# Value products of the last six chunks taken over two chunks, 512 columns at a time

## The chip, the cores and the metric

The kernel runs on one core of a Trainium2 chip. The metric is the time of one execution on the device in microseconds (us), the median of several runs. Engines are named as the profile names them: PE is TensorE (PEld its weight loads), DVE is VectorE, ACT is ScalarE, POOL is GpSimd, SP is SyncE, which issues every transfer.

## The reference

Inputs are `q`, `k`, `v` of 4 batches, 8 heads, 768 positions, 64 values, and per head a decay `lam`. The first half is attention with decay, by blocks of 64 positions and a carried state; the second gates a projection by a causal filter of five taps.

```
for b in range(nb):                       # blocks of 64 positions
    intra = (qb @ kb^T * Dmask) @ vb      # Dmask[i, j] = lam^(i-j), i >= j
    inter = (qb * lam_pow) @ kv_state
    out[b] = intra + inter
    kv_state = lam^64 * kv_state + (kb * rev_pow)^T @ vb
x = out with the heads side by side       # (4, 768, 512)
gate = sigmoid(sum_k conv_w[k] * x shifted by 4 - k positions)
val = x @ w_val                           # 512 x 512, the value products
result = (gate * val) @ w_out             # 512 x 512, the output products
```

The two weights come in float64.

## The kernel before

The work is cut into 12 chunks: chunk i holds 128 positions of two batches (6 chunks for one pair of batches, then 6 for the other). Two chunks in a row make a unit (`UNIT` = 2, six units). Per chunk, TensorE computes the scores (pieces `s`, L470), the intra part (`ia`, L510), the inter part from the state (`in`, L547) and the state's addition (`st`, L572), all in small 64 by 64 products for chunks 3 to 11; VectorE masks the scores (`m`, L490) and updates the state (`up`, L581), GpSimd scales q and k (`qd`, `kd`) and fades the state (`fd`, L584). ScalarE copies the result x out of its bank (`x`, L634).

The second half multiplies in three terms: x is split into a high part (`xh`, ScalarE, L659) and a rest (`xl`, GpSimd, L669), the weights likewise, and a product is high by high, rest by high, high by rest. A value piece `v.i.f` (L734) makes column block f (128 of 512) of chunk i: 12 products whose stationary operand is a 128 by 128 block of the weight and whose moving operand is 256 columns, the 2 x 128 positions of the chunk. Two blocks share a bank. The filter runs per unit and block over 512 elements: the first tap on ScalarE (`t.un.ct.0`, L693), four more on VectorE (`t.un.ct.1` to `4`, L695), then the sigmoid (`sg`, L700). For chunks 6 to 11 (`DIRECT`) the gate is multiplied in place in the bank (`ap`, VectorE, L748), the gated value is cast to its high part (`hh`, ScalarE, L771) and the rest is subtracted (`hl`, VectorE, L774); the bank is free after that. An output piece `p.i.b.j.u` (L797) makes half of the contraction of one batch's 128 positions, moving 512 columns of `w_out`; the evicted bank (`ev`, ACT, L804) is stored by SP (`o`, L807). The very last output is made and stored in two halves of 256 columns.

Order and buffers are written out by hand. `ORDER` (L32) names every piece once, in the order in which all engines get their instructions, and after a colon the buffers that a piece takes (`u0` to `u3` are four of the eight banks, `hs`, `val`, `xs` and others lie in the on-chip buffer). Each engine runs its pieces in that order and waits where a piece needs another engine's result or a buffer not yet free. `Plan.run` (L114) walks the list:

```
        for piece in ORDER.split():
            name, _, takes = piece.partition(":")
            k = self.at[name]
            assert k not in done and done.issuperset(self.work[k][3]), name
```

Of the kernel before, what the change touches and what calls it, by code (L numbers as in the profile page):

```python
# [7 lines left out]
F32 = mybir.dt.float32  # L8
# [4 lines left out]
ALU = mybir.AluOpType  # L13
# [16 lines left out]
H_DVE = (6, 7, 8, 9, 10, 11)  # L30
# [8 lines left out]
xh.1:xs1 wv.1.0.w up.1.0 x.1 qd.2.1:qd1 v.0.1 wv.1.0.v m.2.1.0:A0 wv.1.0.h fd.1.0 m.2.0.0 s.2.1:u3,u1 pb.0.0:val0 xl.1  # L39
# [3 lines left out]
wo.1.1.s wo.0.0.s pb.1.0:val3 qd.3.0:qd1 x.2:x1 wo.1.1.w s.3.0:s0 xh.2:xs0 v.1.2:u1 m.3.1.0:A1 qd.3.1 m.3.0.0  # L43
# [3 lines left out]
wo.0.1.r t.0.3.4 pb.2.1:val2 m.5.1.0:A1 sg.0.0 ia.4.0:xp0 wo.0.1.s xh.3:xs1 in.4.0 wo.0.1.n st.4:u0,u3 sg.0.3 xl.3  # L47
# [6 lines left out]
t.1.2.2 ia.6.0:xp0 p.1.0.0.0:u3 pk.6 t.1.2.3 t.1.3.0:u1 qd.6.0 xh.5:xs1 t.1.3.1 kd.7.0 p.1.0.0.1 t.1.3.2 fd.6.0  # L54
t.1.2.4 in.6.1 ev.1.0.0:o0 m.7.0.0:A1 xl.5 ia.6.1 hh.0.1:hs1 o.1.0.0 t.1.3.3 p.1.1.0.0:u3 ld.8.2:ld2 x.6:x0 up.6.1
ld.8.0 t.1.3.4 t.1.1.0:u2 p.1.1.0.1 hi.2 sg.1.3 t.1.1.1 qd.7.1:qd1 t.1.1.2 v.5.2:u1 ev.1.1.0:o1 fd.6.1 t.1.1.3 hh.0.0
o.1.1.0 ld.9.2:ld1 sg.1.2 qd.7.0 v.5.3 t.1.1.4 ld.9.0 t.1.0.0:u3 sg.1.1 t.1.0.1 hl.0.0 ia.7.0:xp0 pb.5.1:val1 t.1.0.2
in.7.0 st.7:u0,u2 hl.0.1 t.1.0.3 t.1.0.4 p.0.0.0.0:u1 kd.8.1 up.7.0 sg.1.0 ap.2.1 t.2.1.0:u3,g0 fd.7.0 p.0.0.0.1
t.2.1.1 hh.2.1:hs0 m.7.1.0 p.0.1.0.0:u0 ev.0.0.0:o0 ap.2.0 xh.6:xs0 t.2.1.2 p.0.1.0.1 hh.2.0 t.2.1.3 hl.2.0 ap.3.0
v.5.0:u1 ev.0.1.0:o1 t.2.2.0:u0 qd.8.0:qd0 o.0.1.0 t.2.1.4 in.7.1 ia.7.1 t.2.2.1 sg.2.1 s.8.0:s0 hl.2.1 ld.10.0:ld0  # L60
t.2.3.0:u3 t.2.2.2 o.0.0.0 x.7 v.5.1 up.7.1 qd.9.0:qd1 t.2.2.3 p.2.0.0.0:u2 t.2.2.4 pb.5.0 qd.8.1 t.2.3.1 hh.3.0:hs1
sg.2.2 ap.3.1 p.2.0.0.1 kd.8.0 t.2.0.0:u1 m.8.0.0:A0 hh.3.1 t.2.0.1 p.2.1.0.0:u0 ev.2.0.0:o1 kd.9.0 t.2.3.2 o.2.0.0
m.8.1.0 p.2.1.0.1 kd.9.1 t.2.0.2 hl.3.1 t.2.0.3 s.9.0:s0 ev.2.1.0:o0 t.2.0.4 hl.3.0 ia.8.0:xp0 t.2.3.3 in.8.0 sg.2.0
st.8:u2,u0 t.2.3.4 fd.7.1 m.9.0.0:A1 sg.2.3 p.3.1.0.0:u1 qd.9.1 up.8.0 ap.4.0 p.3.1.0.1 hi.3 m.9.1.0 hh.4.0:hs0 fd.8.0
ap.4.1 t.3.1.0:u3,g1 in.8.1 hl.4.0 ev.3.1.0:o1 ia.8.1 t.3.1.1 o.3.1.0 p.3.0.0.0:u2 x.8:x1 ld.11.2:ld2 up.8.1
# [12 lines left out]
sg.4.1 hh.8.1:hs1 p.6.0.0.1 t.5.0.0:u3,g1 hl.8.1 t.5.3.0:u1 v.9.0:u2 t.5.3.1 ev.6.0.0:o0 o.6.0.0 v.9.1 v.8.0:u0 ap.9.0
t.5.3.2 hh.9.0:hs0 v.8.1 hl.9.0 v.9.2:u2 xh.11:xs1 ap.8.0 hh.8.0 v.9.3 hl.8.0 p.8.1.0.0:u0 ap.9.1 hh.9.1 p.8.1.0.1
xh.10:xs0 hl.9.1 t.5.3.3 xl.10 p.9.1.0.0:u2 ev.8.1.0:o0 t.5.3.4 o.8.1.0 t.5.0.1 sg.5.3 o.7.1.0 p.9.1.0.1 t.5.2.0:u0  # L80
xl.11 t.5.2.1 p.8.0.0.0:u1 t.5.2.2 ev.9.1.0:o0 t.5.2.3 p.8.0.0.1 t.5.2.4 p.9.0.0.0:u2 ev.8.0.0:o1 t.5.1.0:u1 o.8.0.0
o.9.1.0 sg.5.2 p.9.0.0.1 t.5.1.1 t.5.1.2 v.11.2:u0 ev.9.0.0:o1 t.5.1.3 o.9.0.0 t.5.0.2 v.11.3 t.5.0.3 t.5.1.4
v.10.2:u2 ap.11.1 t.5.0.4 hh.11.1:hs1 v.10.3 sg.5.1 sg.5.0 v.10.0:u1 ap.10.1 hh.10.1:hs0 v.10.1 v.11.0:u3 ap.10.0
hl.10.1 hh.10.0 v.11.1 hl.10.0 p.10.1.0.0:u2 ap.11.0 hh.11.0 p.10.1.0.1 hl.11.0 hl.11.1 p.10.0.0.0:u1 ev.10.1.0:o0
o.10.1.0 p.10.0.0.1 p.11.1.1.0:u3 ev.10.0.0:o1 p.11.1.1.1 p.11.0.0.0:u0 ev.11.1.1:o0 o.11.1.1 o.10.0.0 p.11.0.0.1
p.11.1.0.0:u2 ev.11.0.0:o0 p.11.1.0.1 o.11.0.0 f.2:u1 ev.11.1.0:o1 o.11.1.0
# [41 lines left out]
def decay_attention_then_gated_conv(  # L128
# [262 lines left out]
    for i in range(N):  # L391
# [256 lines left out]
        xs_buf, hs_buf = Buf("xs"), Buf("hs")  # L648
# [66 lines left out]
    for i, s, un, j, xs_buf, hs_buf, g_buf, t_g, t_xs in gated:  # L715
        gs = lambda u, un=un, j=j: xu[un]["g"][:, HU * u : HU * (u + 1), j]
        t_h, val_buf = {}, Buf("val")
        h_in = i in H_DVE
        assert i >= DIRECT or not h_in
        h_bufs = {}  # L720
        for u in range(2):
            us = slice(HU * u, HU * (u + 1))
            vp_buf = Buf("u")
            h_bufs[u] = vp_buf if h_in else g_buf

            def value(f, u=u, s=s):
                x_hi, x_lo = (s[n].rearrange("p t b i -> p t (b i)") for n in ("x_hi", "x_lo"))
                if f == 0:
                    s["vp", u] = bank("vp", [P, HU, W])
                fs = slice((HU * u + f) * P, (HU * u + f + 1) * P)  # L730
                n_mm = 0
                for ct in range(NT):
                    for w, xx in ((wv.hi, x_hi), (wv.hi, x_lo), (wv.lo, x_hi)):
                        nc.tensor.matmul(  # L734
                            s["vp", u][:, f, :], w[:, ct, fs], xx[:, ct, :],
                            start=n_mm == 0, stop=n_mm == 3 * NT - 1,
                        )
                        n_mm += 1

            def put_by(u=u, us=us, s=s):  # L740
                if "val" not in s:
                    s["val"] = buf("val", "val", [P, NT, W])
                nc.scalar.copy(s["val"][:, us], s["vp", u])

            def apply(u=u, us=us, s=s, i=i, gs=gs):
                val = s["vp", u] if i >= DIRECT else s["val"][:, us]
                s["h", u] = s["vp", u] if i in H_DVE else gs(u)
                nc.vector.tensor_tensor(out=s["h", u], in0=val, in1=gs(u), op=ALU.mult)  # L748

            t_gu = [t_g[ct] for ct in range(HU * u, HU * (u + 1))]  # L750
            t_v = None
            for f in range(HU):
                t_v = add(
                    f"v.{i}.{HU * u + f}", "PE", lambda f=f, g=value: g(f),
                    [t_v, t_xs, *wv.done[HU * u + f], *(t_gu if i >= DIRECT else ())], [vp_buf, xs_buf],
                )
            if i >= DIRECT:
                t_h[u] = add(f"ap.{i}.{u}", "DVE", apply, [t_v, *t_gu], [vp_buf, g_buf])
            else:
                t_v = add(f"pb.{i}.{u}", "ACT", put_by, [t_v], [vp_buf, val_buf])  # L760
                t_h[u] = add(f"ap.{i}.{u}", "DVE", apply, [t_v, *t_gu], [val_buf, g_buf])

        t_hs = []
        for u in range(2):
            us = slice(HU * u, HU * (u + 1))

# [92 lines left out]
```

## Time and profile before

| | |
|---|---|
| median of 3 runs | 209.81 us (209.22 to 210.12) |
| the profiled execution's own time | 209.46 us |
| its span, first to last instruction | 207.7 us |
| TensorE busy | 201.4 us, 97% of the span |
| VectorE, GpSimd, ScalarE busy | 153.6, 116.4, 115.2 us |
| transfers | 36.17 MB, 174 GB/s |

The profile shows one execution. Busy time is when an engine worked; TensorE's products overlap, so the duration of one is longer than the step from its start to the next one's. The chain that ended last follows, back from the end, what released each piece of work. Windows are stretches of the span, in us from its start.

### The profile page before, as it was taken

The numbers are of one execution on the slowest core, as the hardware profiler recorded it, in microseconds if no ns is written. First come the engines' busy times: TensorE is split into PE (matmuls) and PEld (weight loads), VectorE is DVE, ScalarE is ACT, GpSimd is POOL, SyncE is SP. The second block draws the span as 40 slices with busy tenths as digits, with TensorE's granted clock in tenths as the row PEclk, the third lists the DMA queues.
The fourth block names the chain that finished last, engine by engine and source line by source line (L and its number), as shares of the span: only waits on it lengthen the run. The fifth ranks groups of instructions, "written<-read, shape, count | busy, mean of one in ns | idle before, by whom it ended". The sixth has DMA issues, their size and how long they took to land.

```text
span 207.7 us, 7755 instructions
## 1 busy us (share of the span) xinstructions
PE 201.4 (97%) x3460; PEld 179.7 (87%) x3460; DVE 153.6 (74%) x240; ACT 115.2 (55%) x218; POOL 116.4 (56%) x103
## 2 busy tenths in 40 slices
PE   7879899998999999999999999999999999999995
PEld 7569799998999988989797889999789998899883
DVE  5697997989586989999999993465858457683500
ACT  2177779779664967577546394323456336432211
POOL 5176592887887599849999569952440006300000
DMA  5999999703787005985506465120110102220022
GB/s 181 425 419 426 426 429 426 319 6 90 320 300 312 5 3 144 412 358 159 202 3 199 166 218 238 54 104 3 51 54 3 51 0 82 94 81 0 3 95 107
DMA packets 7953, 36.17 MB, mean 174 GB/s; under 512 B 1136, under 2 KB 1392, under 8 KB 4336
## 3 DMA queue, kind: packets, MB, share of 16 engines
q1 hardware_dynamic: 7920, 35.68, 44.6%
q8 instruction: 27, 0.44, 0.9%
q14 instruction: 6, 0.05, 0.1%
HBM read 29.38 MB, written 6.29 MB: 172 GB/s over the span
## 4 chain that ended last, share of the span: by engine, by line
PE 87%; DMA 7%; SPq 2%; DVE 1%; POOL 1%; issue 1%; ACT 0%
PE vp L734 34%; PE op L797 33%; DMA w_raw<-in_w_val 7%; PE xp L510 5%; PE xp L547 4%; PE s L470 4%; PE st L572 4%; SPq L337 1%; PE xp L525 1%; POOL wv_lo L302 1%; PE so L460 1%; PE xp L536 0%; PE st L564 0%; PE fill L205 0%; DVE w_em L260 0%
## 5 line engine op out<-in xcount | busy, mean ns | idle before, releaser
L695 DVE SCALAR_TENSOR_TENSOR acc<-x,conv_sb,acc 128x512 f32<-128x512 f32 x96 | 70.9, 753 | 6.5 <-ACT acc L693 4.7
L797 PE MATMUL op<-wo_hi,hs 128*128 128x512 f32 (+1 forms) x200 | 61.1, 388 | 0.0
L734 PE MATMUL vp<-x_hi,wv_hi 128*128 128x256 f32 x192 | 55.6, 290 | 0.0
L734 PE MATMUL vp<-x_hi,wv_lo 128*128 128x256 f32 x192 | 54.3, 283 | 0.7 <-POOL wv_lo L302 0.7
L734 PE MATMUL vp<-x_lo,wv_hi 128*128 128x256 f32 x192 | 54.2, 282 | 0.0
L797 PEld LDWEIGHTS op<-wo_hi,hs 128*128 128x128 f32 x200 | 36.0, 188 | 7.3
L797 PE MATMUL op<-wo_lo,hs 128*128 128x512 f32 (+1 forms) x100 | 38.4, 384 | 0.0
L734 PEld LDWEIGHTS vp<-x_hi,wv_hi 128*128 128x128 f32 x192 | 36.4, 190 | 1.5 <-issue 0.2
L669 POOL TENSOR_TENSOR x_lo<-x,x_hi 128x1024 fp32r<-128x1024 f32 x10 | 23.9, 2400 | 23.8 <-ACT x_hi L659 23.8
L734 PEld LDWEIGHTS vp<-x_hi,wv_lo 128*128 128x128 f32 x192 | 36.4, 190 | 0.9 <-POOL wv_lo L302 0.9
L734 PEld LDWEIGHTS vp<-x_lo,wv_hi 128*128 128x128 f32 x192 | 36.4, 190 | 0.3
L804 ACT COPY o<-op 128x512 f32<-128x512 f32 (+1 forms) x25 | 14.3, 571 | 24.9 <-PE op L797 23.1
L584 POOL TENSOR_TENSOR sdec<-state,qdec_c 128x512 f32<-128x512 f32 x17 | 19.3, 1138 | 12.0 <-DVE state L581 11.9
L420 POOL TENSOR_TENSOR qd<-ld,qdec_c 128x512 f32<-128x512 f32 (+1 forms) x18 | 23.0, 1286 | 2.6 <-DMA ld<-in_qkv 2.6
L797 PEld LDWEIGHTS op<-wo_lo,hs 128*128 128x128 f32 x100 | 18.8, 188 | 3.9
L700 ACT ACTIVATE g<-acc 128x512 f32<-128x512 f32 x24 | 14.2, 601 | 13.4 <-DVE acc L695 13.2
L774 POOL TENSOR_TENSOR hs<-g,hs 128x512 fp32r<-128x512 f32 x12 | 15.9, 1335 | 8.8 <-ACT hs L771 8.8
L748 DVE TENSOR_TENSOR vp<-vp,g 128x512 f32<-128x512 f32 x12 | 8.4, 699 | 15.5 <-PE vp L734 15.5
L771 ACT CAST hs<-vp 128x512 fp32r<-128x512 f32 x12 | 7.0, 587 | 20.8 <-DVE vp L748 20.8
L693 ACT ACTIVATE acc<-x,conv_sb 128x512 f32<-128x512 f32 x24 | 16.6, 694 | 1.8 <-DVE state L581 1.5
L581 DVE TENSOR_TENSOR state<-st,sdec 128x512 f32<-128x512 f32 x17 | 11.7, 687 | 7.5 <-PE st L572 5.7
L634 ACT COPY x<-xp 128x512 f32<-128x512 f32 x24 | 12.9, 592 | 5.0 <-PE xp L510 4.9
(71 smaller groups left out, 295.7 us busy)
## 6 DMA issues: line engine op xcount, KB each, us to landing
ld<-in_qkv SPq DMA_DIRECT2D x24, 1024.0 KB, 8.4
out<-o SPq DMA_DIRECT2D x23, 256.0 KB, 2.4
w_raw<-in_w_val SPq DMA_DIRECT2D x2, 1024.0 KB, 11.3
w_raw<-in_w_out SPq DMA_DIRECT2D x2, 1024.0 KB, 14.0
out<-o SPq DMA_DIRECT2D x2, 128.0 KB, 1.7
conv_raw<-in_conv_w SPq DMA_DIRECT2D x1, 20.0 KB, 10.4
lam_bc<-in_lam SPq DMA_DIRECT2D x1, 4.0 KB, 1.6
```

The source lines that it names most:

```text
L420: nc.gpsimd.tensor_tensor(out=s["qd"][:, hs, ms], in0=lds[i]["qT"][:, u].rearrange("p h (m i) -> p h m i", m=2)[:, :, ms], in1=qdec[:, hs, ...
L581: nc.vector.tensor_tensor(out=state, in0=s["st"][m], in1=sdec, op=ALU.add)
L584: nc.gpsimd.tensor_tensor(out=sdec, in0=state, in1=qdec_c[:, :, n - 1 : n].to_broadcast([P, H, D]), op=ALU.mult)
L634: nc.scalar.copy(*blocks(s["x"], b))
L669: nc.gpsimd.tensor_tensor(out=s["x_lo"], in0=s["x"], in1=s["x_hi"].bitcast(F32), op=ALU.subtract)
L693: nc.scalar.mul(to, src, w)
L695: nc.vector.scalar_tensor_tensor(out=to, in0=src, scalar=w, in1=to, op0=ALU.mult, op1=ALU.add)
L700: nc.scalar.activation(xu[un]["g"][:, ct].rearrange("p u (b i) -> p b u i", b=NB2), xu[un]["acc", ct].rearrange("p b (u i) -> p b u i", u= ...
L734: nc.tensor.matmul(s["vp", u][:, f, :], w[:, ct, fs], xx[:, ct, :], start=n_mm == 0, stop=n_mm == 3 * NT - 1,)
L774: (nc.vector if h_in else nc.gpsimd).tensor_tensor(out=s["h_lo"][:, us], in0=s["h", u], in1=s["h_hi"][:, us].bitcast(F32), op=ALU.subtract,)
L797: nc.tensor.matmul(s["op", b, j][:, cols], hh[:, ft, ts], w[:, ft, cols], start=ft == 0 and n == 0, stop=ft == NT - 1 and n == 2,)
L804: nc.scalar.copy(s["o", b, j][:, cols], s["op", b, j][:, cols])
```

## The change

The value products of units 3, 4 and 5 (chunks 6 to 11) are made for both chunks of a unit at once. A wide piece `V.un.f` has 12 products of 512 columns into a whole bank, and needs x of both chunks split. The gating, cast and subtraction of a wide group (`apw`, `hhw`, `hlw`) take one column block of both chunks, 512 elements as before. The split x of a unit lies in one tile of twice the size (`xs`), the high part of a unit's gated value in one `hs` buffer, its rest in two `val` buffers. `ORDER` is the same for the first 411 pieces but for the `xs` buffers; from the 412th on (at 104 us in the profile) it is new, for every engine and for SP's stores and loads. `value` is now L728, gating L774, the subtraction L810, the output products L837, the store L847.

```diff
-H_DVE = (6, 7, 8, 9, 10, 11)
+WIDE = (3,4,5)
...
-v.10.2:u2 ap.11.1 t.5.0.4 hh.11.1:hs1 v.10.3 sg.5.1 sg.5.0 v.10.0:u1 ap.10.1 hh.10.1:hs0 v.10.1 v.11.0:u3 ap.10.0
...
+t.5.0.4 sg.5.0 t.5.2.0:u0 xl.11 p.9.1.0.1 t.5.1.4 t.5.2.1 t.5.2.2 t.5.2.3 V.5.0:u3 t.5.2.4 ev.9.1.0:o1 sg.5.1 V.5.1:u2
...
-        def split_x(s=s, now=now, blocks=blocks):
-            at = plan.slot("xs")
-            s["x_hi"] = work.tile([P, NT, NB2, C], F32R, name="x_hi", tag=f"{at}_hi", bufs=1)
-            s["x_lo"] = work.tile([P, NT, NB2, C], F32R, name="x_lo", tag=f"{at}_lo", bufs=1)
+        def split_x(un=un, j=j, s=s, now=now, blocks=blocks):
+            if "x_hi" not in xu[un]:
+                at = plan.slot("xs")
+                for part in ("hi", "lo"):
+                    xu[un][f"x_{part}"] = work.tile(
+                        [P, NT, UNIT, NB2, C], F32R, name=f"x_{part}", tag=f"{at}_{part}", bufs=1
+                    )
+            s["x_hi"], s["x_lo"] = (xu[un][n][:, :, j] for n in ("x_hi", "x_lo"))
...
+    def value(f, to, hi, lo):
+
+        fs = slice(f * P, (f + 1) * P)
+        n_mm = 0
+        for ct in range(NT):
+            for w, xx in ((wv.hi, hi), (wv.hi, lo), (wv.lo, hi)):
+                nc.tensor.matmul(to, w[:, ct, fs], xx[:, ct], start=n_mm == 0, stop=n_mm == 3 * NT - 1)
+                n_mm += 1
...
+        wide, direct = un in WIDE, UNIT * un >= DIRECT
+        if wide and j == 0:
+            continue
...
+        groups = [(f,) for f in range(NT)] if wide else [tuple(range(HU * u, HU * (u + 1))) for u in range(2)]
...
+                if f == fs[0]:
+                    x["vp", j, fs] = bank("vp", [P, len(fs), UNIT, W] if wide else [P, len(fs), W])
...
+                    f"V.{un}.{f}" if wide else f"v.{i}.{f}", "PE", lambda f=f, g=products: g(f),
+                    [t_v, *([gated[n - 1][8]] if wide else []), t_xs, *wv.done[f], *(t_gu if direct else ())], [vp_buf, xs_buf],
...
-    nc = bacc.Bacc("TRN2", target_bir_lowering=False, num_devices=1)
+    nc = bacc.Bacc("TRN2", target_bir_lowering=False, num_devices=1, dynamic_dma_scratch_size=2048)
```

How the order moves is shown at three places. First, TensorE at the value products of the last unit, where they follow output products (`op`). Before:

```order
L797 MATMUL op<-wo_hi,hs 128x512 x2
L797 MATMUL op<-wo_lo,hs 128x512
L734 MATMUL vp<-x_hi,wv_hi 128x256
L734 MATMUL vp<-x_lo,wv_hi 128x256
L734 MATMUL vp<-x_hi,wv_lo 128x256
```

Now:

```order
L837 MATMUL op<-wo_hi,h_hi 128x512
L837 MATMUL op<-wo_hi,h_lo 128x512
L837 MATMUL op<-wo_lo,h_hi 128x512
L728 MATMUL vp<-x_hi,wv_hi 128x512
L728 MATMUL vp<-x_lo,wv_hi 128x512
L728 MATMUL vp<-x_hi,wv_lo 128x512
```

The three value rows repeat: 96 products of 256 columns before, 48 of 512 now. Second, TensorE around the scores of chunk 11 (`s`). Before, they stood between chunk 10's inter part (`xp<-qd,state`) and its state, and value products followed:

```order
L510 MATMUL xp<-A,ld 64x64 x16
L547 MATMUL xp<-qd,state 64x64 x16
L470 MATMUL s<-ld 64x64 x32
L572 MATMUL st<-ld 64x64 x32
L734 MATMUL vp<-x_hi,wv_hi 128x256
L734 MATMUL vp<-x_lo,wv_hi 128x256
L734 MATMUL vp<-x_hi,wv_lo 128x256
```

Now:

```order
L547 MATMUL xp<-qd,state 64x64 x16
L510 MATMUL xp<-A,ld 64x64 x16
L470 MATMUL s<-ld 64x64 x32
L572 MATMUL st<-ld 64x64 x16
L510 MATMUL xp<-A,ld 64x64 x16
L547 MATMUL xp<-qd,state 64x64 x16
L837 MATMUL op<-wo_hi,h_hi 128x512
L837 MATMUL op<-wo_hi,h_lo 128x512
L837 MATMUL op<-wo_lo,h_hi 128x512
```

The first two rows are chunk 10's second half; then chunk 11's scores, its state, its intra part (`xp<-A,ld`, which reads the masked scores A) and its inter part follow each other with nothing between. Third, VectorE from the gating of the second unit from last to the filter of the last (`acc`; a bank's number tells the column blocks apart). Before:

```order
L748 TENSOR_TENSOR vp_2692<-vp_2692,g_2281 128x512
L774 TENSOR_TENSOR hs_2734<-vp_2692,hs_2734 128x512
L695 SCALAR_TENSOR_TENSOR acc_2746<-x_2565,conv_sb_96,acc_2746 128x512
L748 TENSOR_TENSOR vp_2748<-vp_2748,g_2281 128x512
L695 SCALAR_TENSOR_TENSOR acc_2746<-x_2565,conv_sb_96,acc_2746 128x512
L774 TENSOR_TENSOR hs_2792<-vp_2748,hs_2792 128x512
L748 TENSOR_TENSOR vp_2777<-vp_2777,g_2281 128x512
L774 TENSOR_TENSOR hs_2734<-vp_2777,hs_2734 128x512
L748 TENSOR_TENSOR vp_2807<-vp_2807,g_2281 128x512
L774 TENSOR_TENSOR hs_2792<-vp_2807,hs_2792 128x512
L695 SCALAR_TENSOR_TENSOR acc_2746<-x_2565,conv_sb_96,acc_2746 128x512 x2
L695 SCALAR_TENSOR_TENSOR acc_2743<-x_2565,conv_sb_96,acc_2743 128x512
```

Now:

```order
L774 TENSOR_TENSOR vp_2690<-vp_2690,g_2473 128x512
L810 TENSOR_TENSOR h_lo_2717<-vp_2690,h_hi_2703 128x512
L702 SCALAR_TENSOR_TENSOR acc_2737<-x_2500,conv_sb_96,acc_2737 128x512 x2
L702 SCALAR_TENSOR_TENSOR acc_2746<-x_2500,conv_sb_96,acc_2746 128x512 x3
L702 SCALAR_TENSOR_TENSOR acc_2737<-x_2500,conv_sb_96,acc_2737 128x512 x2
L702 SCALAR_TENSOR_TENSOR acc_2746<-x_2500,conv_sb_96,acc_2746 128x512
L702 SCALAR_TENSOR_TENSOR acc_2784<-x_2500,conv_sb_96,acc_2784 128x512 x4
L702 SCALAR_TENSOR_TENSOR acc_2827<-x_2500,conv_sb_96,acc_2827 128x512 x4
L774 TENSOR_TENSOR vp_2814<-vp_2814,g_2736 128x512
```

The last unit's filter began among the gatings of the unit before it; now all its 16 steps stand behind that unit's last subtraction, and all of its own gatings behind them.

## Rows read from the trace of the kernel before

**Rows 1.** The page's first part: span, then busy us of each engine.
```profile
span 207.7 us, 7755 instructions
PE 201.4 (97%) x3460; PEld 179.7 (87%) x3460; DVE 153.6 (74%) x240; ACT 115.2 (55%) x218; POOL 116.4 (56%) x103
```
**Rows 2.** Windows: stretch, its length, busy us of each engine, granted clock, transfers.
```profile
104.40:130.00 25.60, 25.60 (x553) 21.80 (x546) 21.61 (x33) 14.56 (x25) 20.77 (x18) 1.00 0.47 167
130.00:156.00 26.00, 26.00 (x509) 23.09 (x511) 15.95 (x24) 9.95 (x16) 13.63 (x11) 1.00 0.15 53
156.00:182.00 26.00, 26.00 (x196) 23.41 (x187) 16.67 (x24) 12.72 (x21) 4.76 (x2) 1.00 0.14 50
182.00:204.50 22.50, 22.50 (x157) 20.97 (x157) 8.92 (x14) 6.06 (x11) 0.00 (x0) 1.00 0.12 43
```
**Rows 3.** The chain that ended last: start us, us, what, instructions.
```profile
106.50 2.98 PE op L797 x12
...
151.55 0.93 PE st L572 x32
...
159.58 2.75 PE op L797 x12
162.33 8.60 PE vp L734 x72
170.93 11.05 PE op L797 x48
181.98 11.49 PE vp L734 x96
193.47 11.16 PE op L797 x60
```
**Rows 4.** Groups from 104.4 us on: count, busy us, mean ns, idle before.
```profile
L797 PE MATMUL op<-wo_hi,hs 128*128 128x512 f32 x136 | 42.9, 397 | 0.0
L695 DVE SCALAR_TENSOR_TENSOR acc<-x,conv_sb,acc 128x512 f32<-128x512 f32 x51 | 37.7, 753 | 3.9 <-ACT acc L693 2.9
...
L804 ACT COPY o<-op 128x512 f32<-128x512 f32 x17 | 10.0, 588 | 17.8 <-PE op L797 16.1 <-DMA out<-o 1.1 <-ACT x_hi L659 0.6
L748 DVE TENSOR_TENSOR vp<-vp,g 128x512 f32<-128x512 f32 x12 | 8.4, 699 | 15.5 <-PE vp L734 15.5
L693 ACT ACTIVATE acc<-x,conv_sb 128x512 f32<-128x512 f32 x12 | 8.2, 694 | 0.1
L774 DVE TENSOR_TENSOR hs<-vp,hs 128x512 fp32r<-128x512 f32 x12 | 8.2, 690 | 6.1 <-ACT hs L771 6.1
...
L700 ACT ACTIVATE g<-acc 128x512 f32<-128x512 f32 x14 | 8.2, 601 | 7.8 <-DVE acc L695 7.6
L771 ACT CAST hs<-vp 128x512 fp32r<-128x512 f32 x12 | 7.0, 587 | 20.8 <-DVE vp L748 20.8
...
L490 DVE TENSOR_TENSOR A<-s,dmask 128x512 f32<-128x512 f32 x6 | 4.1, 683 | 0.0
...
L470 PE MATMUL s<-ld 64*64 64x64 f32 x144 | 2.6, 218 | 0.0
```
**Rows 5.** Timeline of VectorE from 160 us: start us, us, what.
```profile
160.98 0.69 DVE L774 TENSOR_TENSOR hs<-vp,hs 128x512 fp32r<-128x512 f32 x1 [0.66 <-ACT hs L771]
162.25 0.76 DVE L695 SCALAR_TENSOR_TENSOR acc<-x,conv_sb,acc 128x512 f32<-128x512 f32 x1 [0.58 <-ACT acc L693]
...
165.85 0.75 DVE L695 SCALAR_TENSOR_TENSOR acc<-x,conv_sb,acc 128x512 f32<-128x512 f32 x1
```
**Rows 6.** SP's queue at chunk 11's load, and the page's part on transfers.
```profile
120.49 0.93 SPq L337 DMA_DIRECT2D ld<-in_qkv  x2
...
ld<-in_qkv SPq DMA_DIRECT2D x24, 1024.0 KB, 8.4
```
**Rows 7.** Timeline from 205 us: the last copy.
```profile
204.66 0.37 ACT L804 COPY o<-op 128x256 f32<-128x256 f32 x1 [0.79 <-PE op L797]
```
**Rows 8.** Timeline of VectorE from 92 us.
```profile
92.43 1.73 DVE L748 TENSOR_TENSOR g<-val,g 128x512 f32<-128x512 f32 x1
```

More of the change, by code (lines that the diff above doesn't have):

```diff
@@ L87 @@
+o.10.0.0 o.11.0.0 p.10.1.0.1 ev.10.1.0:o1 o.10.1.0 p.9.0.0.0:u3 p.9.0.0.1 ev.9.0.0:o0 o.9.0.0 p.11.1.1.0:u0 p.11.1.1.1
+ev.11.1.1:o1 f.2:u1 o.11.1.1
 """
@@ L713, in decay_attention_then_gated_conv @@
         gated.append((i, s, un, j, xs_buf, hs_buf, g_buf, t_g, t_xs))
[L715 to L722, printed above, removed]
-            vp_buf = Buf("u")
[L724 to L750, printed above, removed]
@@ L751, in decay_attention_then_gated_conv @@
             t_v = None
-            for f in range(HU):
+            for f in fs:
                 t_v = add(
-                    f"v.{i}.{HU * u + f}", "PE", lambda f=f, g=value: g(f),
-                    [t_v, t_xs, *wv.done[HU * u + f], *(t_gu if i >= DIRECT else ())], [vp_buf, xs_buf],
-                )
[L757 to L761, printed above, removed]
@@ new lines, in split_h_lo @@
+            def split_h_lo(u=u, fs=fs, x=x, direct=direct, wide=wide, j=j):
+                if wide:
+                    if ("lo", u) not in x:
+                        x["lo", u] = buf("val", "h_lo", [P, HU, UNIT, W], F32R)
+                        for jj in range(UNIT):
+                            x["lo", jj, u] = x["lo", u][:, :, jj]
+                    to = x["lo", u][:, fs[0] % HU : fs[0] % HU + 1]
+                else:
+                    to = x["lo", j, u]
+                (nc.vector if direct else nc.gpsimd).tensor_tensor(
+                    out=to, in0=x["h", j, fs], in1=x["to", j, fs].bitcast(F32), op=ALU.subtract
+                )
@@ L782, in decay_attention_then_gated_conv @@
+            t_hhi = add(f"hh{name}", "ACT", split_h, [t_h], [hs_buf, h_buf])
+            t_hlo = add(f"hl{name}", "DVE" if direct else "POOL", split_h_lo, [t_hhi], [hs_buf, h_buf, lo_bufs[u]])
+            for jj in range(UNIT) if wide else (j,):
+                t_hs.setdefault((un, jj), {0: [], 1: []})[u].append(t_hlo)
+    for i, s, un, j_in, xs_buf, hs_buf, g_buf, t_g, t_xs in gated:
+        x, t_h = xu[un], t_hs[un, j_in]
         for b in range(NB2):
@@ L789, in decay_attention_then_gated_conv, with project @@
                 r0 = (NB2 * pair + b) * S + c * C
[L791 removed]
+                def project(u, b=b, j=j, s=s, x=x, j_in=j_in, cols=cols):
                     if u == 0:
@@ L811, in decay_attention_then_gated_conv @@
                     t_p = add(
-                        f"p.{i}.{b}.{j}.{u}", "PE", lambda u=u, g=project: g(u), [t_p, *t_hs[: u + 1], *wo.done[HU * u], *wo.done[HU * u + 1]], [op_buf, hs_buf]
+                        f"p.{i}.{b}.{j}.{u}", "PE", lambda u=u, g=project: g(u), [t_p, *t_h[u], *wo.done[HU * u], *wo.done[HU * u + 1]], [op_buf, hs_buf, x["low", j_in][u]]
                     )
```

140 lines of the change are left out of this document (88 added, 52 removed).

## The prediction

> **What bounds the kernel now.** I read the busy totals first: of a span of 207.7 us TensorE is busy 201.4, the next engine, VectorE, 153.6 [rows 1]. A total does not say that TensorE bounds the part that is changed, so the stretches come next: from 104.4 to 204.5 us, where all the reordered pieces lie, TensorE is busy for the whole of each stretch at a granted clock of 1.00, 2.4 GHz, while VectorE, ScalarE and GpSimd have time left [rows 2]. The chain that ended last is there one unbroken run of TensorE work, and its pieces give what a product costs per instruction, start to start [rows 3]. So the time after 104.4 us is the sum of TensorE's steps, and every other engine counts only where it makes TensorE wait. An instruction's own duration (397 ns for a 512-column output product [rows 4]) is no price: products overlap, and the sum goes by steps.
>
> **What the change does to TensorE.** It removes 288 value products of 256 columns (six chunks, four column blocks, 12 each) and adds 144 of 512 (three pairs, four blocks, 12 each). The columns are the same; what can go is what a product costs above its columns. 72 narrow products took 8.60 us and 96 took 11.49, so 0.1194 and 0.1197, say 0.1196 us each; 48 output products of 512 columns took 11.05, 0.2302 each [rows 3]. No value product of 512 columns is in the trace, but the output product is the same instruction form (128 rows by 128, 512 fp32r columns into one bank), so I take its step. Narrow: 288 x 0.1196 = 34.44 us. Wide: 144 x 0.2302 = 33.15. The difference is 1.29 us, all on the path.
>
> The bounds: 12 output products between two value products took 2.75 us, 0.2292 each [rows 3], and with that step the gain is 1.4 us. The other end is that a wide product costs what two narrow ones do, 0.2392, and then nothing is gained. Less than nothing I exclude: the weights loaded are of the same size and half as many.
>
> TensorE also pays for going from products of 128 rows to the small 64 by 64 ones and back: 12 output products with small ones on both sides took 2.98 us, without them 2.75 [rows 3], so an interruption costs 0.23. After 106.5 us the old order has seven blocks of small products (8b; 9a with scores 10 and state 9; 9b; 10a with scores 11 and state 10; 10b; 11a; 11b), the new one six (inter 8; intra 8 with scores 10, state 9 and 9a; 9b; 10a with state 10; 10b with scores 11, state 11 and 11a; 11b). One less is worth 0.2 us.
>
> **New waits.** I went through each place where the new order puts a consumer nearer to its producer.
> - Chunk 11: its scores, state products and first intra products now stand in one row on TensorE. The intra products need the scores masked: the last score's result (0.22 us, as the 64 by 64 products have it), VectorE's mask at 0.68 [rows 4] and two handovers of some 0.04 (VectorE idles 0.66 over a cast of 0.587 [rows 4, 5]), 0.98 in all; what covers it is the state's 0.93 [rows 3]. Between 0 and 0.1 us is lost; behind the waiting product stand chunk 11's inter products and the output products, which all move with it. I take 0.05. Ahead of the mask on VectorE is the state update of chunk 10, which waits for a GpSimd fade; it ends some 0.8 us earlier by the same durations.
> - Banks: an output product takes the bank of a wide group three times just one wide group later. The group must be gated (0.70), cast (0.59) and subtracted (0.69) [rows 4], with handovers 2.1 us, under the next wide group's 12 x 0.2302 = 2.76. That leaves about 0.5 each time, so I take no wait. It is the cover that the old order has too: the subtraction that ends at 161.67 [rows 5] frees the bank that the value products of the chain's next piece take [rows 3], half a microsecond ahead, and TensorE did not pause.
> - The last pair: its 16 filter steps on VectorE all stand behind the last subtraction of the pair before. From the end of that pair's last wide group TensorE has 48 output products (11.05 us) and three wide groups (8.28) before the group that needs the last gate, 19.3 us. The gate needs the third output product's end (36 x 0.2302 = 8.3), its eviction 0.59, a sigmoid 0.60 and a first tap 0.69 on ScalarE, eight filter steps at 0.79 (0.753 [rows 4] and a handover), a sigmoid 0.60: 17.1 us. It is 2.2 early. No wait.
> - Loads: chunk 11's two stand behind two more stores on SP's queue, behind an eviction that the new order has near 126 us, so that they issue near 127 instead of 120.49 [rows 6]; with 8.4 us to landing [rows 6] they are there at 135.4, and the scores that read them stand near 144. GpSimd waits for one of them, and its next fade is wanted only at 142.
>
> **What I cost at nothing.** Gating, casting and subtracting are 12 instructions each of 512 elements before and after [rows 4]; the splits of x write the same elements into tiles twice as large, and four of their waits for TensorE go; nobody waits for these. The first 411 pieces stand as before, and their instructions wait for nothing new. The scratch setting touches no queue in use: every transfer is issued by SP. The end keeps its form, a half-width output product, its copy of 0.37 us at 204.66 [rows 7] and a 128 KB store.
>
> **The sum.** 1.29 + 0.2 - 0.05 = 1.45, say 1.5 us less. The profiled execution took 209.46 us, 1.8 more than its span; less 1.5 that is 207.96. It stands 0.35 below the median of the three runs, 209.81, which gives 208.31. I predict **208.2 us**.
>
> **Rivals.**
> - *The width is worth nothing.* Then the 9 ns between two narrow steps and a wide one belong to something else that stays, say the weight loads, and only the interruption goes: 209.81 - 0.2 = 209.6 us. For it: no wide value product has been seen. Against: half-width output products run at the narrow step too (60 output products in 11.16 us, 24 of them half as wide: 36 x 0.2302 leaves 0.1197 each [rows 3]), so the step goes with the width, not with the operand. The Trainium skill ("TensorE: Matmul & The Clock Gate", Part 1, on the 56 ns) gives a warm product its columns at 2.4 GHz and a fixed cost of about 2.5 ns; by that rule 144 products fewer save an estimated 0.36 us. The rows give 9 ns, 1.29 us, and speak against the rule.
> - *Waits at the banks give it back.* If the gating chain runs 0.85 us late at the three places with 0.5 to spare, 1.05 returns: 209.3 us. For it: a gating instruction once took 1.73 instead of 0.68 [rows 8]. Against: that was at 92 us, with GpSimd at work beside it; GpSimd is busy 4.76 of 26 us from 156 and not at all from 182 [rows 2].
> - *VectorE becomes the bound in the last pair,* and the kernel is slower. Its filter chain has 2.2 us to spare; TensorE waits for what exceeds that, so it takes 2.2 + 1.5 + 1.05 = 4.7 us of lateness to be 1.05 slower, 210.9 us. For it: the old order began these steps at 162.25 and 165.85 [rows 5], among the value products; the new one begins all after the last subtraction. Against: that lateness is four and more slow instructions such as the one of [rows 8].
>
> **How the numbers follow.** A measurement of this kernel tells about 0.5%, 1.05 us, from no change. Chances: the forecast 0.70; width worth nothing 0.10; waits at the banks 0.14; VectorE's bound 0.06. The first is faster by over 0.5%, the second and third are within it, the last is slower. The range: at the low end the better step (1.4 and 0.2, no mask wait) and a run as far below its median as the fastest shown, 0.59, give 207.6, and 0.2 for what the steps leave open, 207.4; the high end is the first rival's 209.6, which takes in the second. Left out is the slower case, and the edges.
>
> **What would show it.** Right: 144 value products of 512 columns, 12 of them in about 2.76 us in the chain, TensorE busy through every stretch from 104 us, its last output product ending near 203.1 instead of 204.6, the tail of 3 us unchanged. Wrong: a wide step over 0.235 (the first rival); idle time of TensorE before an output product with VectorE's subtraction as releaser (the second); idle time before the last wide groups, released by a sigmoid (the third); idle time over 0.1 us before chunk 11's intra products (the mask).

## The result, and the profile after

The changed kernel takes **207.99 us** (median of 4 runs, 207.53 to 208.27), the kernel before 209.80 beside it: a ratio of 0.9915, with a 95% interval of 0.9886 to 0.9944. The profiled execution took 208.13 us against 209.46. The medians differ by 1.81 us, the two profiled executions by 1.33; with four runs of each kernel, 0.7 to 0.9 us apart among themselves, the runs do not tell these two figures apart, and what follows accounts for the second. In later runs some executions have a granted clock of 0.992 over the span instead of 1.000 and are longer (the kernel before took 209.45 us in the median of 26 at 1.000 and 211.6 in that of 9 at 0.992), so a median depends on how many of them it holds.

The page's first part:

```profile
span 206.4 us, 7456 instructions
...
PE 199.5 (97%) x3316; PEld 172.2 (83%) x3316; DVE 154.5 (75%) x240; ACT 115.2 (56%) x218; POOL 115.3 (56%) x103
```

TensorE has 144 products fewer and 1.9 us less to do [rows 1]; the span is 1.3 us shorter. The windows (stretch, length, busy us of each engine, granted clock, transfers):

```profile
104.40:130.00 25.60, 25.60 (x544) 21.27 (x534) 20.17 (x29) 12.61 (x22) 21.17 (x19) 1.00 0.42 154
130.00:156.00 26.00, 26.00 (x437) 21.73 (x436) 17.87 (x26) 12.32 (x21) 14.46 (x10) 1.00 0.17 66
156.00:182.00 26.00, 26.00 (x174) 21.26 (x173) 19.06 (x29) 12.69 (x22) 2.88 (x3) 1.00 0.14 51
182.00:203.00 21.00, 21.00 (x104) 17.62 (x104) 6.66 (x10) 5.67 (x10) 0.00 (x0) 1.00 0.12 44
```

TensorE is as full as it was [rows 2], at a granted clock of 1.00 (2.4 GHz). So the gain is again a matter of its steps, and the chain that ended last (start us, us, what, instructions) shows them:

```profile
105.58 0.93 PE st L572 x64
106.52 1.57 PE op L837 x6
...
126.33 5.44 PE vp L728 x24
131.78 2.72 PE op L837 x12
...
144.69 1.16 PE s L470 x64
145.85 0.98 PE st L572 x32
146.83 0.60 PE xp L510 x32
...
167.31 11.06 PE op L837 x48
178.37 10.89 PE vp L728 x48
189.25 14.02 PE op L837 x72
203.27 0.86 PE fill L205 x2
```

Read 178.37 against [rows 3]: 48 wide value products take 10.89 us, 0.2269 each, where 96 narrow ones took 11.49. The output products of the row before it keep their step: 11.06 for 48, where it was 11.05. And 12 output products at 131.78 take only 2.72.

Up to chunk 8's state products the two kernels run alike (they start at 105.39 us before, 105.40 after). For all that follows I add TensorE's steps, start to start, by what they make, from the first state product of chunk 8 to the fill at the end. These sums are the instrument of everything below: each is of one profiled execution, and the same pieces in different kernels agree to some 0.05 us, while whole runs spread by 0.5 us and more.

| from chunk 8's state to the fill, us | all | value | output | scores | state | intra, inter |
|---|---|---|---|---|---|---|
| before | 99.08 | 34.80 | 50.94 | 1.87 | 4.17 | 7.31 |
| the change | 97.71 | 33.05 | 51.06 | 2.10 | 4.08 | 7.42 |
| two halves | 101.07 | 34.80 | 51.87 | 1.89 | 4.08 | 8.42 |
| scores first | 97.79 | 33.05 | 51.06 | 1.91 | 4.39 | 7.37 |
| output terms in another order | 97.62 | 33.03 | 51.03 | 2.06 | 4.07 | 7.42 |
| value terms in another order | 97.50 | 33.05 | 51.06 | 1.87 | 4.11 | 7.42 |
| aligned | 96.67 | 33.00 | 50.27 | 1.88 | 4.09 | 7.42 |
| all shifted | 97.50 | 33.05 | 51.06 | 1.87 | 4.11 | 7.42 |
| one interruption less | 98.48 | 33.05 | 50.91 | 1.87 | 5.31 | 7.35 |
| aligned, and one less | 97.56 | 33.01 | 50.04 | 1.88 | 5.30 | 7.35 |
| operands apart | 98.22 | 33.75 | 51.08 | 1.87 | 4.10 | 7.42 |
| before, aligned | 98.77 | 34.88 | 50.54 | 1.87 | 4.17 | 7.31 |
| late filter | 98.90 | 33.21 | 52.09 | 2.11 | 4.08 | 7.42 |
| aligned, rows shared out | 98.26 | 33.01 | 50.04 | 2.54 | 4.11 | 8.56 |

The change, then, won 1.75 us at the value products, and lost 0.12 at the output products, 0.23 at the scores and 0.02 at the rest (0.11 lost at the intra and inter products, 0.09 won at the state).

### The profile page after: what moved, and what is told of

It reads as the page before. It is cut to its first block, busy times and chain, and to the rows that moved or that the text cites. A ratio compares the mean times of both kernels' runs of the same rounds, so it can differ in the third digit from the quotient of the medians.

```text
span 206.4 us, 7456 instructions
## 1 busy us (share of the span) xinstructions
PE 199.5 (97%) x3316; PEld 172.2 (83%) x3316; DVE 154.5 (75%) x240; ACT 115.2 (56%) x218; POOL 115.3 (56%) x103
## 4 chain that ended last, share of the span: by engine, by line
PE 87%; DMA 8%; SPq 2%; DVE 1%; POOL 1%; issue 0%; ACT 0%
PE op L837 33%; PE vp L728 33%; DMA w_raw<-in_w_val 8%; PE xp L510 5%; PE s L470 4%; PE xp L547 4%; PE st L572 4%; SPq L337 1%; PE xp L525 1%; POOL wv_lo L302 1%; PE so L460 1%; PE xp L536 1%; PE st L564 0%; PE fill L205 0%; DVE w_em L260 0%
## 5 line engine op out<-in xcount | busy, mean ns | idle before, releaser
L728 PE MATMUL vp<-x_hi,wv_hi 128*128 128x256 f32 (+1 forms) x144 | 47.3, 328 | 0.0
L728 PE MATMUL vp<-x_hi,wv_lo 128*128 128x256 f32 (+1 forms) x144 | 45.9, 319 | 0.5 <-POOL wv_lo L302 0.5
L728 PE MATMUL vp<-x_lo,wv_hi 128*128 128x256 f32 (+1 forms) x144 | 45.8, 318 | 0.0
L837 PE MATMUL op<-wo_hi,hs 128*128 128x512 f32 x96 | 30.6, 400 | 0.0
L728 PEld LDWEIGHTS vp<-x_hi,wv_hi 128*128 128x128 f32 x144 | 27.3, 190 | 3.1 <-issue 0.2
L728 PEld LDWEIGHTS vp<-x_hi,wv_lo 128*128 128x128 f32 x144 | 27.3, 190 | 2.6 <-POOL wv_lo L302 0.7
L728 PEld LDWEIGHTS vp<-x_lo,wv_hi 128*128 128x128 f32 x144 | 27.4, 190 | 1.9
L837 PEld LDWEIGHTS op<-wo_hi,hs 128*128 128x128 f32 x96 | 17.4, 188 | 3.9
L810 POOL TENSOR_TENSOR hs<-g,hs 128x512 fp32r<-128x512 f32 x12 | 15.4, 1296 | 9.0 <-ACT hs L799 9.0
L837 PE MATMUL op<-wo_hi,h_hi 128*128 128x512 f32 (+1 forms) x52 | 19.7, 379 | 0.0
L837 PE MATMUL op<-wo_hi,h_lo 128*128 128x512 f32 (+1 forms) x52 | 19.6, 377 | 0.0
L837 PE MATMUL op<-wo_lo,h_hi 128*128 128x512 f32 (+1 forms) x52 | 19.6, 376 | 0.0
L837 PE MATMUL op<-wo_lo,hs 128*128 128x512 f32 x48 | 18.8, 392 | 0.0
```

The lines of the kernel that those rows point to most:

```text
L728: nc.tensor.matmul(to, w[:, ct, fs], xx[:, ct], start=n_mm == 0, stop=n_mm == 3 * NT - 1)
L810: (nc.vector if direct else nc.gpsimd).tensor_tensor(out=to, in0=x["h", j, fs], in1=x["to", j, fs].bitcast(F32), op=ALU.subtract)
L837: nc.tensor.matmul(s["op", b, j][:, cols], hh, w[:, ft, cols], start=ft == 0 and n == 0, stop=ft == NT - 1 and n == 2,)
```

## The experiments

My theory at first: the gain is what a value product costs above its columns, 144 times, and the new order itself loses some 0.35 us at chunk 11. The rivals: the order brings the gain; the fixed cost is the 2.5 ns of the Trainium skill's rule ("TensorE: Matmul & The Clock Gate", Part 1).

**Two halves.** Wide groups, banks and order as in the change, but 256 columns at a time:

```diff
-                nc.tensor.matmul(to, w[:, ct, fs], xx[:, ct], ...)
+        for h0 in range(0, to.shape[-1], W):
+            hs = slice(h0, h0 + W)
...
+                    nc.tensor.matmul(to[:, hs], w[:, ct, fs], xx[:, ct, hs], ...)
```

> The changed kernel, with each wide value product issued as two of 256 columns into the two halves of the same bank; the order of all pieces, the buffers and the waits stay those of the change. Theory (the gain is what a value product costs above its columns, some 13 ns, 144 times; the new order itself gives nothing and loses some 0.35 us at chunk 11): twelve wide columns' worth takes 24 x 0.1196 = 2.87 us instead of 2.72, so 48 narrow pairs read 11.5 us in the chain instead of 10.89, and the time goes up by some 1.8 us, to about 209.7 (209.3 to 210.1), no faster than the kernel before. Rival 'the order brings it': stays at 208.0 (207.7 to 208.3). Rival by the Trainium skill's fixed cost of about 2.5 ns a product: 0.36 us more, 208.35.

Measured: 211.06 us, ratio to before 1.004 (1.0001 to 1.0079). The chain:

```profile
147.64 0.71 issue
...
180.87 11.51 PE vp L730 x96
```

and ScalarE's timeline (start us, us, what, idle before):

```profile
177.21 1.19 ACT L846 COPY o<-op 128x512 f32<-128x512 f32 x2 [4.54 <-DMA out<-o]
```

The value products are back at 34.80, to the hundredth what they were before the change. So what the value products gained comes from the width alone. The time is over a microsecond more than I expected; in the profile that is two things which the change's profile does not have: a pause of TensorE of 0.71 us with nothing that released it, in the intra and inter products (1.00 more in all), and an eviction that waited for a slow store, at which the output products lost 0.81. (Three stores issued between 168 and 180 us landed after 4.4 us in the median, five in the change after 2.1.) Without these two the sum would be 99.26, where the kernel before has 99.08: with narrow products the new order is no faster than the old. The time of this run alone would have misled; its steps don't.

**Scores first.** Chunk 11's scores two pieces earlier:

```diff
-up.10.0 apw.3.3 qd.11.0:qd1 in.10.1 ia.10.1 s.11.0:s0 qd.11.1 ...
+up.10.0 apw.3.3 qd.11.0:qd1 s.11.0:s0 in.10.1 ia.10.1 qd.11.1 ...
```

> The changed kernel with the scores of chunk 11 moved ahead of the inter and second intra products of chunk 10, two pieces earlier on TensorE, so that the mask of chunk 11 has the state products, and the two pieces, to finish under. Theory (chunk 11's dense row costs some 0.35 us: scores that read 1.17 us instead of 0.93, and an intra product that waits for the mask): 0.2 to 0.35 us less than the change, about 207.7, with under 0.05 us idle before chunk 11's intra products. Rival (these excesses are only what changing between large and small products costs, wherever it lies): the same as the change, 208.0 within 0.1. Rival (the scores now wait for chunk 11's transposed queries and keys): slower by up to 0.5 us, 208.5, with idle time of TensorE ahead of the scores.

Measured: 208.13 us, ratio to before 0.992 (0.9886 to 0.9953): the same as the change. In the chain:

```profile
145.36 1.08 ACT x L634 x2
146.44 0.04 issue
146.48 0.69 PE xp L510 x32
```

The scores do run without their pause (1.91), but the intra products of chunk 11 now wait for ScalarE, which copies chunk 10's result out of the bank that they write to; the state's sum goes up by 0.31. One wait took another's place. That the scores need to be moved at all fell with the next runs: their 0.23 is missing in the profiles of six kernels in which nothing near them is changed (1.87 or 1.88 in the table) and there in two others (2.06, 2.11), so the order alone does not cause it. Each kernel has one profile, so these can't say whether it goes by the kernel or by the execution; where in TensorE's program it stands is told further down.

**The order of the terms**, to find why an output product of 512 columns steps at 0.2302 us and a value product at 0.2269.

```diff
-for n, (hh, w) in enumerate(((h_hi, wo.hi), (h_lo, wo.hi), (h_hi, wo.lo))):
+for n, (hh, w) in enumerate(((h_hi, wo.hi), (h_hi, wo.lo), (h_lo, wo.hi))):
```

> The changed kernel with the three terms of each output product in another order, so that the high part of h is the stationary operand of two products in a row (high x high, high x low, low x high). It asks why a 512-column output product steps at 0.2302 us and a 512-column value product at 0.2269. Theory (the step depends on whether the stationary operand changes from product to product): the output step falls by a third to a half of the difference or more, to 0.228 or 0.227; some 228 products of 512 columns, so 0.3 to 0.8 us less than the change, 207.2 to 207.7. Rival (it belongs to the operands' place or layout, or to the pieces' shortness): the step stays at 0.2302 and the time at 208.0.

and in another kernel

```diff
-for w, xx in ((wv.hi, hi), (wv.hi, lo), (wv.lo, hi)):
+for w, xx in ((wv.hi, hi), (wv.lo, hi), (wv.hi, lo)):
```

> The changed kernel with the three terms of each value product in another order, so that the stationary operand (a block of the value weights, high or low) changes with every product instead of staying for two. The counterpart of the run on the output products. Theory (a stationary operand that stays saves some 3 to 5 ns a product): the wide step rises from 0.2269 to about 0.230, 12 of them from 2.72 to 2.76, the narrow one from 0.1196 by as much; with 144 wide and some 280 narrow ones 0.5 to 1.2 us more, 208.5 to 209.2. Rival (the operand's change costs nothing): 208.0 and 2.72.

Measured: 208.09 and 208.23 us; 48 output products in 11.05, 48 value products in 10.89. Whether the stationary operand stays for two products makes no difference here. Both theories fell.

**Where the operands lie.** I then looked at single steps of TensorE in the change. Output products have two kinds: a settled 0.2267, and an uneven 0.228 to 0.241 that never settles. Which kind a piece is goes by the buffer that holds h: the first `hs` buffer is quick, the second slow; where only the low part lies in a slow `val` buffer, that half of the contraction alone is slow. In the compiled program the slow buffers begin at 128 modulo 256 bytes, since the x buffers ahead of them are 8,320 bytes long (32 times 256, and 128), and the weights at 0. These addresses stand in no trace; the lengths, and what each pad moves, follow from the kernel. First, all aligned:

```diff
-xu[un]["x"] = buf("x", "x", [P, NP, NB2, HIST + UNIT * C])
+flat = buf("x", "x", [P, NP * NB2 * (HIST + UNIT * C) + 32])[:, : NP * NB2 * (HIST + UNIT * C)]
+xu[un]["x"] = flat.rearrange("p (a b c) -> p a b c", a=NP, b=NB2)
```

> The changed kernel with each x buffer 128 bytes a partition longer, so that the buffers behind them (among them the second one for h and two of the four for its low part) begin at a multiple of 256 bytes in SBUF; no instruction, order or wait is another. In the trace of the change, output products whose stationary operand begins at 128 modulo 256 step at some 0.2326 us, those at a multiple of 256 at 0.2283 or, settled, 0.2267, and 170 of the 269 output products of 512 columns stand by such an operand, against 131 before the change. Theory (the place of the stationary operand sets the step): all settle at 0.2267 after a break, 0.7 to 1.0 us less than the change, 207.1 (206.8 to 207.4), and the output products of the last row but one take 10.9 us for 48 instead of 11.06. Rival (the slow steps belong to the pieces that stand there, not to the address): 208.0, 11.06.

Measured: **207.64 us** (206.85 to 209.04), ratio to before 0.9888 (0.9836 to 0.994). The chain:

```profile
166.49 10.88 PE op L838 x48
177.37 10.88 PE vp L729 x48
188.25 13.77 PE op L838 x72
```

Output and value products now take the same, 0.2267; the output products take 0.79 us less, and the slow scores happen to be missing. Second, everything shifted by 128:

```diff
     conv_sb = const.tile([P, NT, K], F32, name="conv_sb")
+    const.tile([P, 32], F32, name="pad")
```

> The changed kernel with 128 unused bytes ahead of the value weights, so that everything behind is shifted by 128: the value weights, the first buffer for h and two low parts now begin at 128 modulo 256, the second buffer for h and the other two low parts at a multiple. Theory (place of the stationary operand): the wide value product rises from 0.2269 to some 0.2326 us, 48 of them from 10.89 to 11.15, 144 by 0.8 us; of the output products 149 instead of 170 stand slow, 0.1 less; in all 0.7 more, 208.7 (208.4 to 209.0). Rival (value products are quick because of what they are): 10.89, and 208.0.

Measured: 208.04 us, and every step as in the change:

```profile
167.27 11.06 PE op L838 x48
178.33 10.89 PE vp L729 x48
```

My theory was wrong: the value weights now begin at 128 and are as quick as ever. What stayed the same in this run is the distance between the two operands. So, third, the value weights stay and all behind them moves:

```diff
     wv = Weight(w_val, "wv", "g", True)
+    const.tile([P, 32], F32, name="pad")
     wo = Weight(w_out, "wo", "hs", False)
```

> The changed kernel with 128 unused bytes between the value weights and the output weights, so that the value weights stay where they are and everything behind them, x and h among it, lies 128 bytes further. The run that shifted all of it left every step as it was, so the new theory is that a 512-column product is slow where its stationary and its moving operand begin at different places modulo 256 bytes. By it the 143 wide value products, whose x is now 128 off their weights, go from 0.2269 to some 0.2326 us: 48 of them from 10.89 to 11.06 to 11.15, in all 0.5 to 0.8 us more, 208.7 (208.4 to 209.0), and the output products, which keep their distance to h, stay as they were (48 in 11.06). Rival (the value products are quick for another reason, say which of the two operands is the weights): 10.89, 208.0.

Measured: 208.9 us, ratio to before 0.9972 (0.9926 to 1.0017). (The profiled runs of this kernel and of the aligned one before the change had a granted clock of 0.83 from 10 to 20 us, and reach chunk 8 some 1.6 us later; from 108 us on it is 1.00, and I compare from there.) The chain:

```profile
169.25 11.07 PE op L838 x48
180.32 11.15 PE vp L729 x48
```

Now it is the value products that are slow, 0.2323 each, 0.70 us in all (33.75), and the output products are as before. In all these runs a 512-column product is slow where its stationary and its moving operand begin at different places modulo 256 bytes; where either lies by itself does not matter. That the median met the forecast is no support: seven of the ten runs were at a granted clock of 0.992, and the three at 1.000 took 208.10 to 208.22, within the range of the change's runs. The whole times do not show the loss; the finding rests on the steps. Last, the kernel before with the same lengthened x buffers:

> The kernel before the change, with each x buffer 128 bytes a partition longer, as in the aligned run: all its output products then have stationary and moving operand at the same place modulo 256, where 133 of 269 had not. Theory: 133 products by 4 to 5.7 ns, 0.5 to 0.75 us less than the kernel before, 209.0; the aligned change is then 1.5 to 1.9 us quicker than it, by the value products' fixed cost and one interruption alone. Rival (the alignment helped the changed kernel by another way than its output products): no gain here.

Measured: 209.87 us, ratio 1.0003 (0.9964 to 1.0042), so the medians show no gain. Five of the ten runs were at a granted clock of 0.992; the other five took 209.08 in the median, where the kernel before has 209.45. By the steps it is 0.31 us (98.77), 0.40 at the output products less 0.08 at the narrow value products, and less than I expected:

```profile
172.43 10.91 PE op L798 x48
183.33 11.51 PE vp L735 x96
```

Between the two aligned kernels nothing of this is left in the way: 98.77 to 96.67, 2.10 us, of which the value products are 1.88 and the output products 0.27, which I put down to the one interruption less.

**One interruption less.** The second inter product of chunk 8 moved next to the second intra product, on the change (cut from longer lines of `ORDER`):

```diff
-... p.3.1.0.0:u1 m.9.1.0:A1 ap.5.1 in.8.1 up.8.1 p.3.1.0.1 ...
+... p.3.1.0.0:u1 m.9.1.0:A1 ap.5.1 p.3.1.0.1 ...
-... ia.8.1 s.10.0:s0 t.3.1.0:u2,g1 t.3.1.1 hh.4.0 ...
+... in.8.1 ia.8.1 s.10.0:s0 t.3.1.0:u2,g1 t.3.1.1 up.8.1 hh.4.0 ...
```

> The changed kernel with the second inter product of chunk 8 moved behind the 18 output products that follow it, next to the second intra product of chunk 8, and the state update that waits for it with it: one row of small products less among the output products. Theory (an interruption costs 0.09 us at its start, 0.13 at its end and 0.11 in the first large product, by the trace of the change): 0.33 less, 207.7 (207.5 to 207.9). Rival (what the interruption costs is the small products' own time): 208.0. Rival (the state update is late now, chunk 9's inter products wait): 0.2 to 0.6 more than the change, idle time of TensorE near 115 us.

and together with the lengthened buffers:

> The lengthened x buffers and the moved inter product together, on the changed kernel. Theory (both terms are TensorE's steps, which add up): 1.1 to 1.3 us less than the change, 206.8 (206.4 to 207.1), quicker than both kernels. Rival (one of them is given back elsewhere): 207.1 or more.

Measured: 209.04 and 208.2 us, both above what was forecast. The chain of the second:

```profile
112.67 0.93 PE s L470 x64
113.60 0.45 PE st L572 x29
114.05 0.97 issue
115.03 0.74 PE st L572 x34
```

By the steps the interruption was worth 0.30 us on the aligned kernel (output products from 50.27 to 50.04, inter and intra ones from 7.42 to 7.35) and 0.22 on the change itself (51.06 to 50.91, and the same 0.07). But the state products of chunk 9 stop in their midst for 0.97, with nothing that released them. It is not the state update, which my third case named: VectorE has it done at 113.17, ahead of these products. In the last kernel I shared the row out: the scores of chunk 10 go to the next row of small products.

```diff
-... in.8.1 ia.8.1 s.10.0:s0 t.3.1.0:u2,g1 t.3.1.1 up.8.1 hh.4.0 ...
+... in.8.1 ia.8.1 t.3.1.0:u2,g1 t.3.1.1 up.8.1 hh.4.0 ...
-... in.9.1 ia.9.1 sg.3.1 ...
+... in.9.1 ia.9.1 s.10.0:s0 sg.3.1 ...
```

> Lengthened x buffers, the second inter product of chunk 8 moved next to the second intra product as in the run with one interruption less, and the scores of chunk 10 moved from that row of small products to the next one, behind the second intra product of chunk 9 (their mask on VectorE with them, behind two filter steps), so that the row has 192 small products where it had 256 in the runs whose TensorE stood still for 0.97 us in its midst with nothing that released it. Theory (that pause comes with the length of the row): no pause, and one interruption less: 0.2 to 0.33 us less than the aligned run, 207.2 (206.9 to 207.5). Rival (the pause belongs to the state products of chunk 9 or their place in the program): 208.2 as before.

Measured: 208.48 us, no better. The chain, and a row of TensorE's waits (what waited for what, us in total, times, longest):

```profile
113.51 1.16 PE st L572 x64
114.67 0.45 PE xp L510 x29
115.13 0.36 issue
```
```profile
PE st L572 <- DVE state L581: 0.6, 1, 0.6
```

The pause is shorter, 0.36, but in a row of 192 it is still there, and without the scores ahead of them the state products come 0.6 too early for VectorE's update. The theory of the row's length is not borne out as I put it. What the runs do show is the place: in all three the pause follows the 157th small product of the row (32, 32, 64 and 29 with the scores in it; 32, 32, 64 and 29 with the state products in their stead), the same point of TensorE's program, while what stands there differs.

The traces show more of it. From 25 us on TensorE stands still with nothing that released it twenty times in the fourteen profiles, for 0.08 to 0.97 us, and the kernel before has its share:

```profile
47.64 0.35 PE xp L510 x24
47.99 0.59 issue
```

I count TensorE's records in the order of time, products, weight loads and its sequencer's together. Ahead of these pauses stand 1,729 records in all fourteen kernels, 4,801 in the three just named, 6,081 in the run with two halves, 1,473 and 5,825 in one kernel each; all five numbers leave 193 when divided by 256. The slow scores of the change begin at the same place, within five records of the 5,825th, without a whole pause. And each of the twenty ends 1.2 to 1.6 us after a transfer of 16,384 bytes on an instruction queue has ended. The change's page has these transfers:

```profile
q8 instruction: 26, 0.43, 0.8%
```

26 times 256 are 6,656, and the trace has 6,676 records of TensorE. So the pauses go with blocks of 256 of TensorE's instructions, and not with the length of a row or with what stands in it.

**The slower rival's price.** Five additions on VectorE ahead of the last pair's filter, on the change:

```diff
+                        for _ in range(5 if (un, ct, kk) == (5, 0, 1) else 0):
+                            nc.vector.tensor_tensor(out=sdec, in0=state, in1=state, op=ALU.add)
                         nc.vector.scalar_tensor_tensor(
```

> The changed kernel with five more VectorE instructions of 128x512 (an addition whose result nobody reads) ahead of the filter steps of the last pair. It prices the rival that ends on the slower side. In the trace of the change the last sigmoid ends 2.2 us before the last wide group that needs it; five instructions take 3.1 to 3.5 us where VectorE has no gap. Theory (TensorE waits for what exceeds 2.2): 0.9 to 1.3 us more than the change, 209.1, as idle time of TensorE before the last wide groups with a sigmoid as what ends it. Rival (a gap of 1.67 us which VectorE has among the filter steps takes part of it): less, down to nothing, 208.0.

Measured: 209.48 us, ratio to before 1.0 (0.9964 to 1.0037): the gain is gone. TensorE's waits, and the chain:

```profile
PE vp L730 <- ACT g L709: 0.9, 1, 0.9
```
```profile
169.99 0.61 DVE sdec L703
...
178.68 0.60 ACT g L709
...
179.33 11.20 PE vp L730 x48
```

The sum goes up by 1.19 us (98.90), as forecast from a margin of 2.2: five steps of 0.70 are 3.5 late, 1.3 over the margin.

## Why the prediction was right, point by point

**The total** was right: 208.2 forecast, 207.99 measured, and 207.96 forecast for the profiled execution, 208.13 measured. The mechanism was right too: fewer products, and so less of what a product costs above its columns, on a TensorE that is full. That the number came so near is in part luck: one term was too small, and two losses that the prediction does not have made up for it.

**The width: mis-sized.** "The output product is the same instruction form, so I take its step", 0.2302, 1.29 us. The wide value product steps at 0.2269, and the value products gave 1.75. The form was the same, the place of the operands was not: in the kernel before, about half of the output products of 512 columns have their operands apart (the recorded texts count 131 and 133 of 269). Settled, a narrow product takes 0.1200 and a wide one 0.2267, each 13.3 ns above its columns at 2.4 GHz; 144 times 13.3 ns are 1.92, near the 1.88 of the aligned pair.

**The output products: not in the prediction.** I costed them at nothing, since none is added. In the new order 170 have their operands apart, some 40 more, because the parts of h lie in other buffers. Alignment gives the change 0.79 us there and the kernel before 0.40, so the change pays 0.39 more for it. It hid the interruption that was saved.

**The interruption: right**, and a little small: 0.2 forecast, 0.27 in the aligned pair, 0.22 and 0.30 in the two kernels that remove another.

**Chunk 11's mask: right in kind**, 0.05 forecast. The intra products start 0.125 us after the last state product, where these follow each other by 0.03, so some 0.1 is lost. VectorE's mask is the last thing before them:

```profile
145.90 0.69 DVE L490 TENSOR_TENSOR A<-s,dmask 128x512 f32<-128x512 f32 x1 [0.84 <-PE s L470]
```

The 0.23 in the scores beside it is not the mask's; it stands where the pauses shown above stand in TensorE's program, and the prediction has no term for that.

**The sum after the fact:** 1.75, 0.27 and 0.09 (state) won, 0.39, 0.23 and 0.1 lost, is 1.39; the table has 1.37.

**What else I costed at nothing** was nothing. There is no wait at the banks: TensorE's waits from 104 us on are an empty list in the change. The last pair's gate (timeline of ScalarE):

```profile
183.55 0.60 ACT L707 ACTIVATE g<-acc 128x512 f32<-128x512 f32 x1 [2.43 <-DVE acc L702]
```

ends at 184.15, and the fourth group that needs it starts at 186.36: 2.2 early, as forecast. Chunk 11's second load goes out at 127.37, "near 127" in the forecast, and GpSimd waits for it without consequence (timelines of SP's queue and of GpSimd):

```profile
127.37 0.42 SPq L337 DMA_DIRECT2D ld<-in_qkv  x1
```
```profile
133.02 2.52 POOL L420 TENSOR_TENSOR qd<-ld,qdec_c 128x512 f32<-128x512 f32 x2 [2.03 <-DMA ld<-in_qkv]
```

**The rivals.** "The width is worth nothing" is refuted by the run with two halves, which gives back all of the 1.75 us at the value products; what else it lost has other causes, named there. The Trainium skill's rule ("TensorE: Matmul & The Clock Gate", Part 1, a fixed cost of about 2.5 ns) disagrees with the trace, which has 13.3 ns for these fp32r products; the measurement decides. Waits at the banks did not come. VectorE as the bound in the last pair is a real limit, 2.2 us away, and the run with the late filter shows its price beyond that point.

**Faster than both kernels** is the change with lengthened x buffers, by its steps: 1.04 us less than the change, of which 0.79 is the alignment. In whole times the two intervals, 0.9836 to 0.994 and 0.9886 to 0.9944, overlap, so those alone would not tell it.

## What to carry to other kernels

When the bounding engine is full, cost a change by the steps of that engine, and before you take a step from another instruction of the same form, see whether all of that form step alike: here half of them did not. Wider products save a fixed cost per instruction, but new buffers move operands, and that alone cost 0.39 of the 1.75 us that the width brought. A small gain is shown by sums of steps of unchanged pieces, not by whole times; the run with two halves was over a microsecond off for reasons of its own.

## What the runs showed of the hardware

- A product of 512 fp32r columns steps at 0.2267 us where stationary and moving operand begin at the same place modulo 256 bytes (both at 0, or both at 128), and at about 0.2325 where they are 128 apart. Products of 256 columns are not slower for it: from 60 us on they step at 0.1188 in the kernel with the operands apart and at 0.1198 in the change (means between two value products). Only the distances 0 and 128 occur here.
- Going from 128-row products to a row of small ones and back costs 0.22 to 0.30 us, by the kernels with one interruption less.
- TensorE pauses at times with nothing that released it, twenty times in the fourteen profiles, each time after a number of its records that leaves 193 modulo 256, and 1.2 to 1.6 us after an instruction transfer of 16,384 bytes has ended. All but one of the twenty stand in rows of small products, where a step is 7 to 40 ns. The Trainium skill ("Runtime: NRT & Kernel Launch", Instruction fetch mechanics) says that an engine's instructions are fetched in blocks of 256 while it runs; the trace agrees, with 26 such transfers for 6,676 records. That the pauses are waits for these blocks is a strong argument from place and order; no run here moves that place on purpose.
